# Gated linear attention into a gated SSM on one Trainium2 core: all small tiles of a turn in one cluster, TensorE's program filled to three fetch blocks a turn, loads behind the cluster

## The chip, the cores and the metric

The kernel runs on one core of one Trainium2 chip. The metric is the device time of one execution in microseconds (us); the median of three runs of the kernel before is 269.57 us (269.48 to 269.81). All views below come from one execution that the hardware profiler recorded; it took 269.61 us itself.

Engines: PE is TensorE's matmul stream (PEld its weight loads, PEq its sequencer), DVE is VectorE, ACT is ScalarE, POOL is GpSimd, SP is SyncE, which here only issues DMA.

## The reference

Two blocks follow each other, all in fp32, with B=4, H=8, S=768, D=48, 384 = H·D and 512 inner channels:

```python
# q, k, v, alpha: (B, H, S, D)
for t in range(S):
    state = alpha[:, :, t, :, None] * state + einsum('bhd,bhe->bhde', k[:, :, t], v[:, :, t])
    y[:, :, t] = einsum('bhd,bhde->bhe', q[:, :, t], state)
x = y.transpose(0, 2, 1, 3).reshape(B, S, H * D)
proj = x @ w_in                       # 384 x 1024
val, gate = proj[..., :512], proj[..., 512:]
for t in range(S):
    h = exp(A_log) * h + val[:, t, :]
    ys[:, t, :] = h
out = (gate * sigmoid(gate) * ys) @ w_out   # 512 x 384
```

## The kernel before

The 4 x 768 positions are cut into N = 12 groups of 256, three to a batch; one pass of the main loop over n is a turn. A group consists of two chunks of 128 (c) or four subchunks of 64 (u, L = 64). The recurrence of the first block is done per subchunk, in matrix form: `scan_P` forms the running product P of alpha, `scan_V` the same backwards, and with them q and k are scaled into Zq and Zk. What a turn works on is spread over three groups: turn n projects group n, finishes the attention of group m = n+1, and starts that of m+1.

TensorE's work in a turn, in the order of before:

- `project(n, cc)` for cc = 0..3 (L989): the product of x with w_in, 24 matmuls 128x128 by 128x256, each run as two passes. Each cc gives a half pv (the value) and a half pg (the gate). DVE scans pv into hh (L996), ACT makes silu of pg (sg, L1007), and POOL multiplies the two into f_last (L1009).
- `third(m)`: products of Zq with the carried state sums (`carried`, L848) and of the masked scores with v within a subchunk pair (`values(m, False)`, L835); `join` then copies y to yst and moves it by DMA into xT, the next projection's right-hand side.
- `scores(m+1)` (L799): 64 matmuls of 48x64 by 48x112 in two halves, of Zk with Zq; the result is masked by DVE (L814) into A and copied by ACT to AK, of which POOL masks a part (L819), and to K.
- `output_parts(n)` (L1072): the product of f with w_out by seven instead of eight half-products (S1 to S4, T1 to T4 are sums of quarters of f and of w_out). S3 and S1 (L1056, L1059) are made on POOL, S2 (L1060) and S4 (L1061) on DVE, behind the last f; DVE (L1100 to 1102) and POOL (L1098, L1103) combine the products. It is a generator: each `next(outs)` issues a piece.
- `second(m+1)`, issued at the head of the next turn: `values(m+1, True)` (L835) and `states` (L867), behind which ACT evicts the states and POOL adds them up (`add_up`, L885, L887).

The stages for 48x64 and 64x64 tiles are called small below; projection and outputs use full 128x128 tiles. In a turn of before there are two clusters of small work: third with scores, and, behind the outputs, values with states.

DVE's preparations for later groups come from the generator `products(l)`, of which `go(k)` issues the next k steps: transpose of alpha (al, L601), of k, `scan_P` (L636), a junk read on ACT with `scan_V` (L655), Zk (L620), transpose of q, Zq (L611). No scheduler reorders anything: instructions run on each engine in the order in which this code issues them (`manual_schedule`). Which PSUM bank a product gets is written out by hand, as a string of digits (`taken`).

The first turns (n = 0, 1) have an order of their own; the diff's main part is the branch of n >= 2.

Of the kernel before, what the change touches and what calls it, by code (L numbers as in the profile page):

```python
# [343 lines left out]
FLOOR = 1e-31  # L344


@with_exitstack
def fast(
# [128 lines left out]
    As, Ks = [A0, AK[:, :, :, D:]], [K0, AK[:, :, :, 0:L]]  # L477
# [184 lines left out]
    def products(m):  # L662
# [21 lines left out]
                 "23012301" "230132" "01230123" "012310" "23012301" "230132" "01230123" "012310"  # L684
                 "23012301" "230132" "01230123" "012310" "23012301" "230132" "01230123" "012310"
                 "23012301" "0132" "01320132" "0132")

    def bank(tag=None):
        if tag:
            return ps_at.tile([C, 512], FP32, tag=tag, name=tag)  # L690
        return ps_mm.tile([C, 512], FP32, tag=f"mm{next(taken)}", name="mm")
# [111 lines left out]
    def masks(m, cs=range(G), between=None):  # L803
        sc = [[t[:, 0:4 * (L + D)].rearrange("p (h x) -> p h x", h=4) for t in pair] for pair in scs[m]]
        mb = mask[:, None, :]
        if m < NG:
            for c in cs:
                for i in range(2):
                    nc.vector.tensor_mul(As[i][:, c], sc[c][i][:, :, D:], mb.to_broadcast([C, 4, L]))
                for i in range(2):  # L810
                    nc.scalar.activation((K0, dS[m % 2][1])[i][:, c, :, 0:D], sc[c][i][:, :, 0:D], AF.Copy)
            return
        for c in range(G):
            nc.vector.tensor_mul(A0[:, c], sc[c][0][:, :, D:], mb.to_broadcast([C, 4, L]))  # L814
            nc.scalar.activation(AK[:, c], sc[c][1], AF.Copy)  # L815
        if between:
            between()
        t = AK.rearrange("p c h x -> p (c h) x")[:, :, D:]
        nc.gpsimd.tensor_mul(t, t, mb.to_broadcast([C, G * 4, L]))  # L819
        for c in range(G):  # L820
            nc.scalar.activation(K0[:, c, :, 0:D], sc[c][0][:, :, 0:D], AF.Copy)

    def values(m, across):

        v_sb = vs[m % NV]
        if across:
            ys[m] = [t.rearrange("p (e t) -> p e t", e=2) for t in bank_pair("y")]
        for c in range(G):
            for e in range(2):
                for h in range(2):  # L830
                    i = 1 - h if across else h
                    for s in range(2):
# [3 lines left out]
                                         v_sb[rows, c, 4 * i + p, :], As[i][rows, c, p, :],  # L836
# [15 lines left out]
    def states(m):  # L852
# [7 lines left out]
        for c in range(G):  # L860
            for p in range(4):
                for h in range(2):
                    if c < n[h]:
                        rows = ds(L * h, L)
                        for i in range(2):
                            to = st[h][ds(64 * i, D), c, p, :] if m else st[h][c][ds(64 * i, D), p, :]
                            nc.tensor.matmul(to, ((K0, dS[m % 2][1]) if m < NG else Ks)[i][rows, c, p, 0:D],  # L867
# [6 lines left out]
        for h in range(2):  # L874
            nc.scalar.activation(parts[h][:, 0:n[h], :, 0:D], st[h][:, 0:n[h]], AF.Copy)  # L875
# [99 lines left out]

    def project(n, cc, late=False, between=None):
# [10 lines left out]
        def passes(part):  # L987
            for vg, kk in part:
                nc.tensor.matmul((pv, pg)[vg], w_ins[cc][:, kk, vg, :], xT[:, kk, :],  # L989
                                 start=(kk == 0), stop=(kk == NK - 1))  # L990

# [83 lines left out]
    def output_parts(n):  # L1075
# [11 lines left out]
        yield  # L1087
# [125 lines left out]
    def second(m):  # L1213
        if m < N:
            values(m, True)
            states(m)
            add_up(m, (0, 1, 2))

    def third(m):
        if m < N:  # L1220
            carried(m, (1,))
            values(m, False)
            carried(m, (0, 2, 3))
            return join(m, [nc.sync, nc.gpsimd])

    late = (1,)
    for n in range(N):
# [37 lines left out]
        elif n == 1:  # L1265
# [29 lines left out]
            f2()  # L1295
            output(0)
# [8 lines left out]
        else:  # L1305
            if n == 2:
                first(m)
            if n - 1 not in late:
                go(1)
                if n == N - 2:  # L1310
                    check_w(5)
                next(outs, None)
                second(m)
                go(1)
                if n == N - 2:
                    check_w(0)
            else:
                go(1)
            f0 = project(n, 0)
            f0()  # L1320
            if n == N - 2:
                check_w(1)
            if n == 2:
                go(1)
            load_raw("a", n + 3, nc.sync)
            load_raw("k", n + 3, nc.sync)
            if n != 2:
                go(1)
# [3 lines left out]
            if n - 1 in late:  # L1332
                second(m)
            if n == 2:
                go(1)
# [10 lines left out]
            load_raw("q", n + 3, nc.sync)  # L1346
# [3 lines left out]
            f3 = project(n, 3)  # L1350
            f3()
            if m + 1 < N:
                go(1)
# [6 lines left out]
            rest = third(m)  # L1360
            if n < N - 1:
                outs = output_parts(n)
            if n not in late and m + 1 < N:
                scores(m + 1)
                masks(m + 1, between=lambda: next(outs))
                next(outs)
                rest()
                add_up(m, (3,))
                next(outs)
                go(1)  # L1370
                if n == N - 3:
                    check_w(4)
            else:
                if m < N:
                    next(outs)
                    next(outs)
                    rest()
                    add_up(m, (3,))
                if n < N - 2:
                    go(1)  # L1380
                    for _ in outs:
                        pass
            load_v(m + 2, nc.sync)
# [4 lines left out]
        if n == N - 2:  # L1388
            for _ in outs:
                pass  # L1390
        if n > 1 and n in late:
# [54 lines left out]
```

## Time and profile before

| quantity | value |
|---|---|
| median of three runs | 269.57 us (269.48 to 269.81) |
| the profiled execution | 269.61 us |
| its span, first to last instruction | 267.9 us |
| granted TensorE clock | 1.000 |
| DMA packets, moved | 52304, 41.19 MB |

Lines of the profile name the engine, the line of the code, the operation and out<-in by the program's names. "busy" is the time in which an engine's instructions ran, and what stands in brackets behind a timeline row is the engine's idle time ahead of it and what released it. q8 is the queue that brings instructions. In the chain of waits, each row is a piece of the chain: start in us, length in us, engine, tile and line, and the number of passes.

The busy tenths of PE and POOL in 40 slices of the span show the shape of the run: a ramp, the steady turns, and an end in which POOL has less to do.

```profile
PE   7999999999999999999999999999999999999994
POOL 8221314084168997995985995996876986646010
```

### The profile page before, as it was taken

To read this page: it belongs to the slowest core of one execution; us is meant where nothing else is said; L and a number is where in the kernel's file an instruction comes from. 1 tells how busy PE (TensorE), PEld (TensorE's weight loads), DVE (VectorE), ACT (ScalarE), POOL (GpSimd) and SP (SyncE) were. 2 spreads that over 40 slices of the span, in tenths; PEclk is the share of its full clock that TensorE was granted. 3 is DMA by queue.
4 is the path that set the end of the run, shared out by engine and by line. 5 is a ranking of instruction groups with operands and counts; after the bars stand their busy time and mean duration, and the time that the engine had idled before them with its cause. 6 is when DMAs were issued, how large, how long until landed. Compare 5 with 4: busy or idle time off the path is not lost.

```text
span 267.9 us, 10005 instructions
## 1 busy us (share of the span) xinstructions
PE 262.4 (98%) x4172; PEld 230.5 (86%) x4172; DVE 236.9 (88%) x326; ACT 111.9 (42%) x272; POOL 166.0 (62%) x186
## 2 busy tenths in 40 slices
PE   7999999999999999999999999999999999999994
PEld 5998889877688988988988988988988989988984
DVE  7979998996999999999999998999999998883462
ACT  4667766372242642532533524524524515214021
POOL 8221314084168997995985995996876986646010
PEclk9999999999999999999999999999999999999999
DMA  5948984896993669559697488569598501201101
GB/s 177 307 141 262 287 187 152 227 209 149 271 219 82 133 164 223 122 146 221 132 230 165 104 218 184 125 160 216 128 209 174 144 2 29 76 2 38 68 7 60
DMA packets 52304, 41.19 MB, mean 154 GB/s; under 512 B 27392, under 2 KB 50944, under 8 KB 52256
## 3 DMA queue, kind: packets, MB, share of 16 engines
q1 hardware_dynamic: 49472, 37.53, 57.8%
q0 software_dynamic: 1536, 2.20, 3.2%
q10 hardware_dynamic: 1248, 0.79, 1.1%
q8 instruction: 34, 0.56, 0.9%
q14 instruction: 14, 0.11, 0.1%
HBM read 32.54 MB, written 4.72 MB: 139 GB/s over the span
## 4 chain that ended last, share of the span: by engine, by line
PE 91%; DVE 2%; DMA 2%; issue 1%; ACT 1%; POOL 1%; ACTq 0%; DVEq 0%; POOLq 0%
PE mm L989 47%; PE mm L1072 18%; PE y L835 4%; PE y L848 4%; PE mm L1023 4%; PE s L799 4%; PE mm L799 3%; PE s L867 3%; DMA raw_q<-in_q_dram 2%; PE mm L708 1%; PE mm L704 1%; PE mm L703 1%; DVE P L636 1%; PE mm L751 1%; POOL w_in L557 1%
## 5 line engine op out<-in xcount | busy, mean ns | idle before, releaser
L989 PE MATMUL mm<-xT,w_in 128*128 128x256 f32 x576 | 129.2, 382 | 0.1
L989 PEld LDWEIGHTS mm<-xT,w_in 128*128 128x128 f32 x576 | 108.0, 190 | 15.8 <-POOL w_in L557 0.4
L1007 ACT ACTIVATE sg<-mm 128x256 f32<-128x256 f32 x48 | 18.4, 383 | 88.8 <-PE mm L989 84.4
L1009 POOL TENSOR_TENSOR f_last<-sg,hh 128x256 f32<-128x256 f32 x36 | 28.3, 794 | 26.1 <-ACT sg L1007 22.6
L887 POOL TENSOR_TENSOR sum<-sum,dS 128x192 f32<-128x192 f32 x30 | 39.7, 1325 | 3.0 <-ACT dS L875 1.4
L636 DVE TENSOR_TENSOR_SCAN P<-al,lower 128x1028 f32<-128x1028 f32 x12 | 30.7, 2562 | 0.3
L996 DVE TENSOR_TENSOR_SCAN hh<-a_dec,hh,mm 128x256 f32<-128x256 f32 x32 | 23.3, 729 | 8.3 <-PE mm L989 7.8
L655 DVE TENSOR_TENSOR_SCAN V<-al,ends 128x1028 f32<-128x1028 f32 x12 | 28.5, 2375 | 0.4
L964 POOL DMA_DIRECT2D xT<-yst x44 | 22.5, 517 | 5.1 <-ACT yst L961 3.7
L557 POOL TENSOR_TENSOR w_in<-w_in,wr 128x768 int32<-128x768 int32 x4 | 7.3, 1823 | 25.5 <-DVE wr L552 16.1
L1072 PE MATMUL mm<-wide,wr 128*128 128x192 f32 x120 | 23.0, 327 | 0.0
L1072 PEld LDWEIGHTS mm<-wide,wr 128*128 128x128 f32 x120 | 20.0, 190 | 0.0
L601 DVE STREAM_TRANSPOSE k<-raw_k 128x1024 f32<-128x1024 f32 x9 | 18.5, 2054 | 0.0
L601 DVE STREAM_TRANSPOSE q<-raw_q 128x1024 f32<-128x1024 f32 x9 | 18.3, 2030 | 0.0
L875 ACT ACTIVATE dS<-s 128x384 f32<-128x384 f32 (+1 forms) x18 | 7.4, 461 | 24.4 <-PE s L867 24.4
L1072 PE MATMUL mm<-w_out,f_last 128*128 128x192 f32 x80 | 17.4, 340 | 0.0
L819 POOL TENSOR_TENSOR AK<-AK,mask 128x512 f32<-128x512 f32 x9 | 13.7, 1522 | 5.9 <-ACT AK L815 5.7
L601 DVE STREAM_TRANSPOSE al<-raw_a 128x1024 f32<-128x1024 f32 x8 | 16.4, 2052 | 0.0
L620 DVE TENSOR_TENSOR Zk<-k,V 128x1024 f32<-128x1024 f32 (+1 forms) x14 | 16.0, 1146 | 0.3 <-ACT k L715 0.3
L611 DVE TENSOR_TENSOR Zq<-q,P 128x1024 f32<-128x1024 f32 (+1 forms) x14 | 15.7, 1120 | 0.0
L848 PEld LDWEIGHTS y<-Zq,sum 48*64 48x64 f32 x656 | 11.6, 134 | 3.5 <-issue 3.2
L835 PE MATMUL y<-A,v 64*64 64x64 f32 x352 | 14.5, 221 | 0.0
(196 smaller groups left out, 502.5 us busy)
## 6 DMA issues: line engine op xcount, KB each, us to landing
out_dram<-o_sb SPq DMA_DIRECT2D x23, 192.0 KB, 2.3
v<-in_v_dram SPq DMA_DIRECT2D x22, 192.0 KB, 4.1
raw_k<-in_k_dram SPq DMA_DIRECT2D x18, 184.0 KB, 5.2
raw_q<-in_q_dram SPq DMA_DIRECT2D x18, 184.0 KB, 5.4
raw_k<-in_k_dram SPq DMA_DIRECT2D x18, 176.0 KB, 5.4
raw_q<-in_q_dram SPq DMA_DIRECT2D x18, 176.0 KB, 5.4
wbits<-in_moe_w_in_dram SPq DMA_DIRECT2D x8, 384.0 KB, 4.9
raw_a<-in_alpha_dram SPq DMA_DIRECT2D x16, 184.0 KB, 3.9
```

Of the source, the lines that this page charges most:

```text
L601: nc.vector.transpose(out=by_runs(to).rearrange("p h c j -> p h j c"), in_=raws[name][:, 0:4 * ROW].rearrange("p (h j d) -> p h j d", h=4, ...
L636: nc.vector.tensor_tensor_scan(out=P, data0=al[:, 0:4 * GP], data1=lower.rearrange("p h t -> p (h t)"), initial=0.0, op0=ALU.mult, op1=ALU ...
L655: nc.vector.tensor_tensor_scan(out=V[:, ::-1], data0=al[:, 1:4 * GP + 1][:, ::-1], data1=ends.rearrange("p h t -> p (h t)")[:, ::-1], init ...
L799: nc.tensor.matmul(scs[m][c][i][ds(L * h, L), ds(p * (L + D), L + D)], Zk[rows, c, p, ds(h * L, L)], Zq[rows, u, p], start=True, stop=True ...
L835: nc.tensor.matmul(ys[m][i][ds(64 * s, 64), e, ds(c * C + h * L, L)], v_sb[rows, c, 4 * i + p, :], As[i][rows, c, p, :], start=across and ...
L848: nc.tensor.matmul(ys[m][i][ds(64 * s, 64), e, ds(u * L, L)], Ss[j][rows, p, :], Zqs[m % 2][rows, u, p, D:], start=False, stop=True, skip_ ...
L887: nc.gpsimd.tensor_add(Ss[j][:, :, 0:D], Ss[j - 1][:, :, 0:D], part)
L964: engines[n % len(engines)].dma_start(out=xT[to, a], in_=st[rows, i, e])
L989: nc.tensor.matmul((pv, pg)[vg], w_ins[cc][:, kk, vg, :], xT[:, kk, :], start=(kk == 0), stop=(kk == NK - 1))
L996: nc.vector.tensor_tensor_scan(out=hh, data0=a_dec[:, cc:cc + 1].to_broadcast([C, GC]), data1=pv, initial=prev_h[cc][:, GC - 1:GC] if n % ...
L1009: f = lambda: engine.tensor_mul(fs[n][cc], sg, hh)
L1072: nc.tensor.matmul(o, a[:, k], b[k] if type(b) is list else b[:, k], start=start and k == 0, stop=k == KC - 1, skip_group_check=True)
```

## The change

The order of a turn is changed, the program of PE gets empty instructions, and the loads move.

- **Order.** Behind project cc = 3 come `scores(m+1)` with its masks, then `third(m)`, and in the same cluster `states(m+1)` and `values(m+1, True)`; then the outputs. For m = 5 and 8 (`apart`) values and states stay behind the outputs. `states` hands back its eviction, issued behind an output piece; `add_up` follows.
- **Empty instructions.** `fill` spreads `FILL[n]` NO_OPs over the 24 projection matmuls of turns 1 to 9, 989 in all.
- **Buffers.** A0 and AK alternate between two places each (the second in wobits[0]); POOL's mask is two instructions, one behind each of ACT's copies; y and mm banks are handed out from one string, with "a" and "b" for the y banks.
- **Loads.** k for a later group at the head of the turn, v behind the last piece of the outputs of the turn before, q and alpha behind the cluster.
- **DVE.** Zq is ahead of the last hh, V behind the first hh.

```diff
+FILL = {1: 78, 2: 79, 3: 128, 4: 128, 5: 96, 6: 128, 7: 128, 8: 96, 9: 128}
...
+    def A_of(m):
+        n = m % 2 if m > NG else 1
+        return A0s[n], AKs[n][:, :, :, D:]
...
         for c in range(G):
-            nc.vector.tensor_mul(A0[:, c], sc[c][0][:, :, D:], mb.to_broadcast([C, 4, L]))
-            nc.scalar.activation(AK[:, c], sc[c][1], AF.Copy)
-        if between:
-            between()
-        t = AK.rearrange("p c h x -> p (c h) x")[:, :, D:]
-        nc.gpsimd.tensor_mul(t, t, mb.to_broadcast([C, G * 4, L]))
-        for c in range(G):
+            nc.vector.tensor_mul(A0s[m % 2][:, c], sc[c][0][:, :, D:], mb.to_broadcast([C, 4, L]))
+            nc.scalar.activation(AKs[m % 2][:, c], sc[c][1], AF.Copy)
             nc.scalar.activation(K0[:, c, :, 0:D], sc[c][0][:, :, 0:D], AF.Copy)
+            t = AKs[m % 2][:, c, :, D:]
+            nc.gpsimd.tensor_mul(t, t, mb.to_broadcast([C, 4, L]))
...
-            ys[m] = [t.rearrange("p (e t) -> p e t", e=2) for t in bank_pair("y")]
+            ys[m] = [t.rearrange("p (e t) -> p e t", e=2) for t in bank_pair("y" if m <= NG else None)]
...
+    def fill(n, cc, i):
+        count = FILL.get(n, 0)
+        at = 2 * NK * cc + i
+        return count * (at + 1) // 24 - count * at // 24
...
                 nc.tensor.matmul((pv, pg)[vg], w_ins[cc][:, kk, vg, :], xT[:, kk, :],
                                  start=(kk == 0), stop=(kk == NK - 1))
+                for _ in range(fill(n, cc, NK * vg + kk)):
+                    nc.tensor.nop(hint="fill", nofuse=True)
...
-    late = (1,)
+    apart = (5, 8)
...
             if n == 2:
-                first(m)
-            if n - 1 not in late:
                 go(1)
-                if n == N - 2:
-                    check_w(5)
+            else:
+                if m + 1 < N:
+                    go(1)
+                    load_raw("k", n + 3, nc.sync)
+                go(1)
                 next(outs, None)
-                second(m)
-                go(1)
-                if n == N - 2:
-                    check_w(0)
-            else:
-                go(1)
+                load_v(m + 1, nc.sync)
+            if n == N - 2:
+                check_w(5)
             f0 = project(n, 0)
             f0()
+            go(1)
...
-            f3 = project(n, 3)
+            h3, f3 = project(n, 3, True)
+            if m + 1 < N:
+                go(1)
+            h3()
             f3()
             if m + 1 < N:
-                go(1)
+                scores(m + 1)
+                masks(m + 1)
...
-            rest = third(m)
-            if n < N - 1:
+            if m < N:
+                rest = third(m)
+                load_raw("q", n + 3, nc.sync)
+                if m + 1 < N and m not in apart:
+                    evict = states(m + 1)
+                    values(m + 1, True)
+                go(1)
+                if n + 3 < N:
+                    load_raw("a", n + 4, nc.sync)
+                rest()
                 outs = output_parts(n)
-            if n not in late and m + 1 < N:
-                scores(m + 1)
-                masks(m + 1, between=lambda: next(outs))
                 next(outs)
-                rest()
-                add_up(m, (3,))
+                if m + 1 < N and m not in apart:
+                    evict()
                 next(outs)
-                go(1)
...
+                if m in apart:
+                    values(m + 1, True)
+                    states(m + 1)()
+                if m + 1 < N:
+                    add_up(m + 1)
```

How the instructions move, first on DVE around the end of a turn, from the transpose of q on. Before (L601 is the transpose, L611 Zq, L996 hh, L1060 S2, L1061 S4, L814 the masks, L636 P):

```order
L601 STREAM_TRANSPOSE q<-raw_q 128x4x8x32
L996 SCALAR_TENSOR_TENSOR hh<-a_dec,mm 128x256
L611 TENSOR_TENSOR Zq_117<-q,P 128x4x4x64
L996 SCALAR_TENSOR_TENSOR hh<-a_dec,mm 128x256
L601 STREAM_TRANSPOSE al_130<-raw_a 128x4x8x32
L1060 TENSOR_TENSOR wr<-f_last,wr 128x256
L1061 TENSOR_TENSOR wr<-f_last,wr 128x256
L814 TENSOR_TENSOR A_114<-s_2520,mask 128x256
L814 TENSOR_TENSOR A_114<-mm,mask 128x256
L601 STREAM_TRANSPOSE k<-raw_k 128x4x8x32
```

The same place of the change (L613 the transposes, L623 Zq, L1019 hh, L831 the masks into the second A, L1083 and L1084 S2 and S4):

```order
L1019 SCALAR_TENSOR_TENSOR hh<-a_dec,mm 128x256
L613 STREAM_TRANSPOSE q<-raw_q 128x4x8x32
L623 TENSOR_TENSOR Zq_117<-q,P 128x4x4x64
L1019 SCALAR_TENSOR_TENSOR hh<-a_dec,mm 128x256
L831 TENSOR_TENSOR wobits_104<-s_3097,mask 128x256
L831 TENSOR_TENSOR wobits_104<-mm,mask 128x256
L1083 TENSOR_TENSOR wr<-f_last,wr 128x256
L1084 TENSOR_TENSOR wr<-f_last,wr 128x256
L613 STREAM_TRANSPOSE al_130<-raw_a 128x4x8x32
L613 STREAM_TRANSPOSE k<-raw_k 128x4x8x32
```

Zq stands directly behind q's transpose, and the transpose of al, S2 and S4 have moved from ahead of the masks to behind them.

Then PE at the end of the projection in the change (L1010 the projection's matmuls, L816 the scores, whose place was taken by third before):

```order
L1010 MATMUL mm<-xT,w_in_99 128x256
L1013 NO_OP x5
L1010 MATMUL mm<-xT,w_in_99 128x256
L1013 NO_OP x6
L816 MATMUL s_2322<-Zq_117,Zk 64x112
L816 MATMUL s_2323<-Zq_117,Zk 64x112
L816 MATMUL s_2322<-Zq_117,Zk 64x112
```

Behind every projection matmul stand five or six empty instructions, and the first product behind the projection reads Zq of the group two turns ahead.

More of the change, by code (lines that the diff above doesn't have):

```diff
@@ L1295, in fast @@
             f2()
+            check_w(4)
             output(0)
@@ L1387, in fast @@
             output(n)
[L1388 to L1391, printed above, removed]
             first(m + 1)
```

77 lines of the change are left out of this document (31 added, 46 removed), and 5 rows, old and new, of the table taken.

## Prediction

> **What bounds the kernel now.** I read the page first: the busy shares, the chain that ended last and the queues.
>
> ```profile
> span 267.9 us, 10005 instructions
> PE 262.4 (98%) x4172; PEld 230.5 (86%) x4172; DVE 236.9 (88%) x326; ACT 111.9 (42%) x272; POOL 166.0 (62%) x186
> PEclk9999999999999999999999999999999999999999
> q8 instruction: 34, 0.56, 0.9%
> PE 91%; DVE 2%; DMA 2%; issue 1%; ACT 1%; POOL 1%; ACTq 0%; DVEq 0%; POOLq 0%
> ```
>
> TensorE (PE) is busy for 98% and holds 91% of the chain at full clock, VectorE (DVE) is busy for 88%. An 88% over the whole span hides the ramp and the tail, so next come the busy times over seven steady turns, from the start of scores(4) to that of scores(11), and over three single turns.
>
> ```profile
> 86.58:224.28 137.70, 137.70 (x2269) 124.07 (x2264) 132.78 (x149) 54.74 (x140) 113.85 (x120) 1.00 0.69 156
> sum 58.98, PE 58.98 PEld 53.15 DVE 56.59 ACT 23.36 POOL 48.12; mean PE 19.66 PEld 17.72 DVE 18.86 ACT 7.79 POOL 16.04
> ```
>
> The columns of the first row are the window, its length and then PE, PEld, DVE, ACT, POOL. PE never stops: 137.70 of 137.70, 19.67 us a turn. But DVE works 132.78 of those 137.70, so it has only 4.92/7 = 0.70 us of slack a turn. PE is the bound with a second engine right behind it. Anything that ties the two more tightly must be held against that 0.70.
>
> What PE does in one turn is read from the chain of waits (start, length, what), and what DVE does from its timeline (start, length, line, operands).
>
> ```profile
> 107.86 4.75 PE mm L1072 x28
> 112.61 0.62 PE y L835 x32
> 113.23 0.70 PE s L867 x48
> 113.94 10.56 PE mm L989 x48
> 124.49 0.39 PE y L848 x16
> 124.89 0.47 PE y L835 x32
> 125.35 0.70 PE y L848 x48
> 126.05 0.77 PE s L799 x32
> 126.82 0.77 PE mm L799 x32
> ...
> 145.56 0.77 PE s L799 x32
> ```
> ```profile
> 127.64 0.42 DVE L814 TENSOR_TENSOR A<-mm,mask 128x256 f32<-128x256 f32 x1 [0.18 <-PE mm L799]
> 127.98 2.05 DVE L601 STREAM_TRANSPOSE k<-raw_k 128x1024 f32<-128x1024 f32 x1
> 129.87 2.69 DVE L636 TENSOR_TENSOR_SCAN P<-al,lower 128x1028 f32<-128x1028 f32 x1
> 138.70 2.02 DVE L601 STREAM_TRANSPOSE q<-raw_q 128x1024 f32<-128x1024 f32 x1
> 140.58 0.66 DVE L996 TENSOR_TENSOR_SCAN hh<-a_dec,hh,mm 128x256 f32<-128x256 f32 x1
> 141.18 1.17 DVE L611 TENSOR_TENSOR Zq<-q,P 128x1024 f32<-128x1024 f32 x1
> 142.98 0.75 DVE L996 TENSOR_TENSOR_SCAN hh<-a_dec,hh,mm 128x256 f32<-128x256 f32 x1 [0.63 <-PE mm L989]
> 143.64 2.04 DVE L601 STREAM_TRANSPOSE al<-raw_a 128x1024 f32<-128x1024 f32 x1
> 145.56 0.42 DVE L1060 TENSOR_TENSOR wr<-f_last,wr 128x256 f32<-128x256 f32 x1
> 146.02 0.84 DVE L1061 TENSOR_TENSOR wr<-f_last,wr 128x256 f32<-128x256 f32 x1
> 146.78 0.41 DVE L814 TENSOR_TENSOR A<-s,mask 128x256 f32<-128x256 f32 x1
> ```
>
> The reader is to see where the slack lies: once before the last hh (0.63, for the projection) and once before the second mask (0.18, for the scores). From the second mask at 127.64 to the end of Zq at 142.35 DVE runs 14.71 us without a gap. And Zq ends at 142.35, while the scores that read it start at 145.56, after the projection and third: this lead of 3.2 us is what the change spends.
>
> **The merged cluster.** Values and states used to be a small cluster of their own between outputs and projection. Changing tile size costs PE: values took 0.62 behind outputs and 0.47 inside a cluster, 0.15 more. For the way back, the last turn's projection, with no small tile ahead of it, gives the number:
>
> ```profile
> 242.45 0.39 PE y L848 x16
> 249.07 7.12 PE mm L989 x33
> 249.94 9.50 PE mm L989 x44
> 259.44 4.99 PE mm L1072 x28
> ```
>
> 44 passes in 9.50 are 0.216 a pass, so 48 take 10.36, and a projection behind small tiles takes 10.56: 0.20 more. A cluster less saves 0.15 + 0.20 = 0.35 us. Six turns are merged (groups 4, 5, 7, 8, 10, 11 by the change's own index, all but 6 and 9): 6 x 0.35 = **−2.1 us**, if PE stays the bound. A merged turn on PE alone would be 19.66 − 0.35 = 19.31.
>
> **The scores brought forward.** In the order of before, PE ran third (0.39 + 0.47 + 0.70 = 1.56) between the projection and the scores; now the scores are right behind the projection, and their masks come ahead of S2, S4 and the al transpose on DVE. So DVE's work that used to cover PE's third and scores now stands behind the masks, and while PE computes scores, DVE has only hh and the first mask. That closes a loop through both engines: Zq, scores, second mask, all the rest of DVE's turn, Zq again. Its length, step by step:
>
> - second mask to the end of Zq, the unbroken stretch: 14.71
> - S2 and S4, now inside it (145.56 to 146.78): 1.22
> - al's transpose, now inside it (143.64 to 145.56): 1.92
> - Zq directly behind q rather than behind an hh: q ends at 140.72 and the hh started at 140.58, so that overlap is lost: 0.14
> - both halves of scores, 0.77 + 0.77 and some 0.05 for the change of tile: 1.59
> - two handovers, Zq to PE and PE to mask (126.82 + 0.77 to 127.64 is 0.05): 0.10
>
> The sum is 19.68 us a turn, against PE's 19.31. The hh and first mask cost nothing extra: 0.66 + 0.37 lies inside the 1.69 of scores and handovers, the rest of it, 0.66, is DVE idling. The loop alone is back at the pace of before: the 0.35 saved on PE is gone. Behind the waiting scores stand, on PE, third, states, values and the outputs; all become late by the wait, and join's copies and the output evictions on ACT with them, but none of these is in the loop.
>
> **Collisions with GpSimd.** On top come DVE and POOL in each other's way. S2 and S4 are the same operation on tiles of one size; the view of their line shows minimum, median and maximum in ns:
>
> ```profile
> L1060 DVE TENSOR_TENSOR wr<-f_last,wr x9: 424/426/480, 88.0 to 243.8; 128x256 f32<-128x256 f32 x9
> L1061 DVE TENSOR_TENSOR wr<-f_last,wr x9: 424/836/840, 88.5 to 244.2; 128x256 f32<-128x256 f32 x9
> L636 DVE TENSOR_TENSOR_SCAN P<-al,lower x12: 2277/2544/3274, 6.4 to 208.4; 128x1028 f32<-128x1028 f32 x12
> 134.26 2.07 POOL L885 COPY sum<-dS 128x192 f32<-128x192 f32 x1 [0.64 <-ACT dS L875]
> ```
>
> S4 is 424 alone and 836 beside POOL's S1; P is 2277 to 3274, which I put down to POOL too; a POOL copy of 128x192 takes 2.07 while V runs. The Trainium skill, page "SBUF — State Buffer", section "SBUF: two separate sides", says that VectorE with two SBUF inputs and GpSimd hold their shared port exclusively, one waiting for the other's whole instruction; these three rows agree. In the changed order S2 and S4 meet POOL's S1 and two mask pieces, P meets wide_S and the sums. The best case, both freed, is S4 −0.42 and P 2.69 − 2.28 = −0.41: −0.8 a turn. The worst is S2 doubled too (+0.42) and P at its longest (3.27 − 2.69 = +0.58): +1.0. I take +0.4, one more doubled operation, since the splitting of POOL's mask puts one more POOL instruction next to DVE's two SBUF operations. A merged turn is then 20.1 us.
>
> **The apart turns.** Two of the seven loops hold a group that stays apart (5 and 8 as index m): PE pays the change of tile there (0.35), so the projection's first part is later, and hh of its first block, which now stands ahead of V, waits for it. I take +0.3: 20.4.
>
> **Loads, buffers, banks.** Second A and AK, the y banks' use, moved loads: no engine time is added. A load is read once in some 20 us and lands in 3.9 to 5.4 (queue rows: KB, us to landing):
>
> ```profile
> raw_q<-in_q_dram SPq DMA_DIRECT2D x18, 184.0 KB, 5.4
> raw_a<-in_alpha_dram SPq DMA_DIRECT2D x16, 184.0 KB, 3.9
> ```
>
> The k load moves to the head of the turn, v behind the outputs' last part, q behind the join's DMAs, all on SP's queue, each still well ahead of its reader in the order. I take 0; the worst, one landing time of 5.4 in one turn, would still lie within the forecast's own range. The V scan behind hh does not change the length of the loop.
>
> **The empty instructions.** 989 of them on PE's program, 5.3 for each of 24 matmuls a turn. The nearest row is PE's own semaphore instruction:
>
> ```profile
> L989 PEldq EVENT_SEMAPHORE  x37: 51/51/51, 22.0 to 248.6; - x37
> ```
>
> 5.3 x 51 = 272 ns, and a projection matmul (two passes) takes 432: hidden under the matmuls already queued; **0**. Should the sequencer not run ahead, all show: 989 x 0.051 = +50 us. I take 0, as PE's semaphores cost no gap in the row of the seven turns. What the fill is for, fetch, costs nothing before: 34 blocks, and PE 137.70 of 137.70 busy. The Trainium skill, page "Runtime: NRT & Kernel Launch", section "Instruction fetch mechanics", says the engine fetches its next block while it executes and that crossing a block is mostly hidden; by that rule fill and cluster alike are worth 0 and the sum stays as it is.
>
> **The sum.** Seven loops: 5 x 20.1 + 2 x 20.4 = 141.3, against 137.70: +3.6. The first scores wait behind Zq once, +0.1. The last merged group lies behind the last scores: −0.35. Together +3.3 on the profiled execution's span of 267.9: 271.2; with the 1.7 us outside the span (269.61 − 267.9), 272.9. The median of the runs is 0.04 below that execution. Forecast: **273.0 us**. Its own range follows from the collision bounds. At +0.0 in the five merged loops and 20.1 in the apart ones: 5 x 19.68 + 2 x 20.1 = 138.6, so +0.9 + 0.1 − 0.35, 270.3. At +1.0 everywhere: 5 x 20.68 + 2 x 20.98 = 145.4, so +7.7 − 0.25, 277.0.
>
> **The rivals.**
>
> *PE stays the bound* (the other side). If the collisions fall by 0.4 or more a turn (S4 free of S1), the loop is 19.68 − 0.4 = 19.28, under PE's 19.31; then the −2.1 stands: 267.5 (two apart turns then stay on PE too). For it: S4 collides in nearly every turn now, and 0.4 is one such collision. Against it: the POOL pieces move with S2 and S4, not away from them.
>
> *A wash.* Collisions as now and apart turns no dearer than merged ones: 7 x 19.68 = 137.8, +0.1 + 0.1 − 0.35: 269.5. For it: nothing in the loop is new work; against it: it needs two terms at zero at once.
>
> *Fetch stalls in the large cluster.* Scores, third, states and values are 480 instructions in 1.54 + 1.56 + 0.70 + 0.47 = 4.3 us: 9 ns each, where the projection needs 216 ns for two. A block of 256 goes by in 2.3 us; the q8 row gives 0.9% x 16 x 267.9 / 34 = 1.1 us of transfer for one. For it: the margin is thin, and the change shapes the program by blocks. Against it: 34 blocks and no gap. Price: one transfer's 1.1 a turn over six turns, in part under the DVE loop: some +3 on the forecast, 276.
>
> *The empty instructions are not hidden:* 269.6 + 50 = 320. Or they never reach the chip: then q8 stays at 34 packets, and nothing else moves, since they are costed at 0.
>
> **How the numbers follow.** The forecast 0.55, PE as the bound 0.22, the wash 0.10, fetch stalls 0.07, the empty instructions' price 0.06. A measurement of this kernel can tell about 0.2%, 0.5 us, from no change. Faster 0.22, same 0.10, slower 0.68. The range that should hold the time reaches down over the rival on the other side and up over the forecast's own bounds and the first fetch stalls: 267.2 to 277.0.
>
> **What would show it.** Right: PE's busy share of the steady turns falls below 100%, with PE's scores waiting for DVE's Zq, DVE idling some 0.3 to 0.7 before the masks, and the turn at 20 us; values inside the cluster at 0.47, and six projections at 10.36; q8 at 34 + 989/256, about 38 packets; the projection's passes still 0.216. Wrong: PE at 100% in the steady turns (collisions fell), gaps on PE inside the cluster with no engine as releaser (fetch), or projections longer than 10.56 (empty instructions). S4 at 424 in the changed trace would mean that the collision term has the wrong sign.

## The result and the profile after

The changed kernel takes 283.83 us (median of four runs, 283.43 to 284.6), the kernel before 269.52 us on the same chip: ratio 1.0534, interval 1.0507 to 1.0562. The forecast of slower holds, but the loss is 14.3 us where 3.4 were forecast, and the time lies outside the range. The profiled execution of the changed kernel took 284.6 us with a span of 282.9, against 267.9 before.

The page of the changed kernel: busy shares, the queue that brings instructions (packets, MB, share), and the chain.

```profile
PE 264.6 (94%) x4172; PEld 232.7 (82%) x4172; DVE 238.6 (84%) x326; ACT 112.6 (40%) x272; POOL 158.9 (56%) x195
q8 instruction: 37, 0.61, 0.9%
PE 52%; DVE 30%; issue 6%; DMA 6%; ACT 2%; SPq 1%; POOL 1%; DVEq 0%; ACTq 0%; POOLq 0%
```

PE's chain share fell from 91% to 52%, DVE's rose from 2% to 30%, and 6% is "issue": an engine that waits for nothing the profile shows. The same seven turns as in the prediction, scores(4) to scores(11) (window, length, then PE, PEld, DVE, ACT, POOL):

```profile
86.46:236.52 150.06, 138.50 (x2245) 124.94 (x2245) 133.37 (x147) 55.37 (x140) 107.41 (x126) 1.00 0.65 147
```

They take 150.06 instead of 137.70 us, 12.36 more of the span's 15.0. PE works 0.8 longer and stands still for 11.56, where it never did. PE's waits over the whole span (what waited, for what: us in total, times, longest) tell it in two parts:

```profile
PE s L816 <- DVE Zq L623: 4.4, 8, 0.8
PE mm L862 <- issue: 4.2, 4, 1.3
PE y L862 <- issue: 3.9, 4, 1.1
PE mm L1095 <- issue: 0.4, 1, 0.4
PE y L1095 <- issue: 0.4, 1, 0.4
```

The first row is the wait that the prediction forecast, eight times, 0.55 us each. The two L862 rows are a stop that it had costed at nothing: 8.1 us, eight times, in the middle of third. (The two rows of 0.4 us lie in the outputs of the two apart turns, at no block's end, and come back in many runs below; they are not counted as stops.) The chain of one merged turn shows where (start, length, what):

```profile
105.92 1.24 DVE Zq L623
107.16 0.14 issue
107.30 1.00 PE s L816 x32
108.29 0.77 PE mm L816 x32
109.06 0.23 PE mm L862 x16
109.29 0.47 PE mm L849 x32
109.76 0.23 PE mm L862 x15
109.98 1.34 issue
111.33 0.70 PE mm L862 x33
112.03 0.69 PE s L881 x46
112.71 0.52 PE y L849 x32
113.24 4.75 PE mm L1095 x28
117.98 1.24 PE mm L1010 x6
119.22 5.56 DMA raw_k<-in_k_dram
```

32 + 32 + 16 + 32 + 15 = 127 passes, then 1.34 us of nothing, inside a run of equal matmuls on the same operands. It is pass 127 in all eight turns (127 passes are 254 weight loads and matmuls). The last row names a load of k, and the page's chain has 6% of DMA for such rows, but no engine is seen waiting for it: DVE, whose timeline follows, does not idle for more than 0.04 us at a time between 119.32 and 129.37. A stop also costs more than its gap: 33 carried passes behind it show 0.70 us, as many as 48 took in one piece before, and the first half of the scores behind its wait shows 1.00 instead of 0.77. That is some 0.2 us each time.

DVE's timeline behind that stop:

```profile
117.44 0.35 DVE L1122 TENSOR_TENSOR wr<-wide,mm 128x192 f32<-128x192 f32 x1 [0.36 <-PE mm L1095]
...
119.32 0.75 DVE L1019 TENSOR_TENSOR_SCAN hh<-a_dec,hh,mm 128x256 f32<-128x256 f32 x1 [0.87 <-PE mm L1010]
119.98 0.16 DVE L665 RECIPROCAL ends<-P 128x4 f32<-128x4 f32 x1
120.17 2.30 DVE L667 TENSOR_TENSOR_SCAN V<-al,ends 128x1028 f32<-128x1028 f32 x1
...
127.49 1.23 DVE L623 TENSOR_TENSOR Zq<-q,P 128x1024 f32<-128x1024 f32 x1
128.63 0.74 DVE L1019 TENSOR_TENSOR_SCAN hh<-a_dec,hh,mm 128x256 f32<-128x256 f32 x1
129.90 0.42 DVE L831 TENSOR_TENSOR wobits<-s,mask 128x256 f32<-128x256 f32 x1 [0.53 <-PE s L816]
130.66 0.42 DVE L831 TENSOR_TENSOR wobits<-mm,mask 128x256 f32<-128x256 f32 x1 [0.34 <-PE mm L816]
```

The first hh waits for PE's projection, V stands behind it, and Zk, q and Zq behind V. So PE's stop arrives at Zq, and Zq holds the next scores: a loop through both engines, 107.30 to 128.86, 21.56 us.

### Where the blocks begin

PE's records (weight loads, matmuls, empty instructions, semaphores), counted in order of start, put the stop in all eight turns exactly 256 records behind the first record of scores, its wait for Zq; the numbers of both leave 193 when divided by 256. So a block of 256 is taken to begin at each such number. Against these blocks stand the 16 KiB packets of queue q8 (one packet a block, an estimate: before, PE has 8,452 records and q8 34 packets, 249 a packet). For three blocks of the changed kernel that begin with scores, and three of the kernel before that begin in a cluster (us):

```
kernel   block starts, lasts   packet starts, takes   next block runs
after    107.19  4.14          108.43  1.42           111.33
after    128.75  3.87          130.36  0.93           132.62
after    151.29  3.75          152.40  1.38           155.04
before   104.93  2.27          104.23  1.35           107.21
before   144.16  2.28          142.85  1.38           146.44
before   183.40  2.13          179.66  1.34           185.53
```

A block of small tiles can pass in 2.1 to 2.3 us; before, its successor's packet had been started ahead of it. In the changed kernel the packet starts 1.1 to 1.6 us into the block and PE goes on 1.3 to 1.5 us after it is over. No such block lasts less than 3.6 us.

The same count over all 20 traces, the runs below included, from 25 to 260 us, gives 620 blocks, with the packets put to the blocks in their order. None begins sooner than 1.2 us after its packet is over. PE idles at 97 of the ends for 1.2 to 1.7 us after a packet; the other idling at an end is another wait, longer after the packet. Of the 82 blocks whose last record starts less than 2.75 us after their first, as only small tiles do, 19 have the next packet started at most 0.1 us into the block, and none of them ends in a stop; the other 63, with the packet 0.2 us or more into the block, all do. Of the 484 blocks of 4 us and more, 12 end in a stop.

### The profile page after: what moved, and what is told of

Read it like the earlier page. It is cut to its first block, busy times and chain, and to the rows that moved or that the text cites. A ratio compares the mean times of both kernels' runs of the same rounds, so it can differ in the third digit from the quotient of the medians.

```text
span 282.9 us, 11027 instructions
## 1 busy us (share of the span) xinstructions
PE 264.6 (94%) x4172; PEld 232.7 (82%) x4172; DVE 238.6 (84%) x326; ACT 112.6 (40%) x272; POOL 158.9 (56%) x195
## 4 chain that ended last, share of the span: by engine, by line
PE 52%; DVE 30%; issue 6%; DMA 6%; ACT 2%; SPq 1%; POOL 1%; DVEq 0%; ACTq 0%; POOLq 0%
PE mm L1010 14%; PE mm L1095 14%; DVE q L613 6%; DVE V L667 6%; DMA raw_k<-in_k_dram 5%; DVE hh L1019 5%; DVE Zq L623 4%; PE s L816 3%; PE mm L816 3%; PE y L1095 3%; PE s L881 3%; PE y L862 2%; DVE P L648 2%; PE y L849 2%; DVE Zk L632 2%
## 5 line engine op out<-in xcount | busy, mean ns | idle before, releaser
L1010 PE MATMUL mm<-xT,w_in 128*128 128x256 f32 x456 | 103.6, 382 | 0.1
L1010 PEld LDWEIGHTS mm<-xT,w_in 128*128 128x128 f32 x456 | 85.5, 190 | 12.4 <-POOL w_in L569 0.4
L1032 POOL TENSOR_TENSOR f_last<-sg,hh 128x256 f32<-128x256 f32 x36 | 40.3, 1121 | 33.1 <-DVE hh L1019 21.9
L980 POOL DMA_DIRECT2D xT<-yst x44 | 22.5, 517 | 12.7 <-ACT yst L977 12.4
L1010 PE MATMUL y<-xT,w_in 128*128 128x256 f32 x120 | 27.5, 379 | 0.0
L1019 DVE TENSOR_TENSOR_SCAN hh<-a_dec,hh,mm 128x256 f32<-128x256 f32 x26 | 19.2, 738 | 8.1 <-PE mm L1010 8.1
L1010 PEld LDWEIGHTS y<-xT,w_in 128*128 128x128 f32 x120 | 22.8, 190 | 3.1
L903 POOL TENSOR_TENSOR sum<-sum,dS 128x192 f32<-128x192 f32 x30 | 18.6, 621 | 2.0
L613 DVE STREAM_TRANSPOSE k<-raw_k 128x1024 f32<-128x1024 f32 x9 | 18.2, 2024 | 0.0
L613 DVE STREAM_TRANSPOSE q<-raw_q 128x1024 f32<-128x1024 f32 x9 | 18.2, 2024 | 0.0
L1120 POOL TENSOR_TENSOR wide_S<-wide_S,wr 128x192 f32<-128x192 f32 x9 | 15.1, 1674 | 5.6 <-ACT wr L1103 5.5
L1095 PE MATMUL mm<-wide,wr 128*128 128x192 f32 x88 | 17.2, 327 | 0.4 <-issue 0.4
L816 PEld LDWEIGHTS s<-Zq,Zk 48*64 48x64 f32 x384 | 9.6, 133 | 8.5 <-PE y L1010 3.6
L613 DVE STREAM_TRANSPOSE al<-raw_a 128x1024 f32<-128x1024 f32 x8 | 16.4, 2050 | 0.0
L816 PE MATMUL s<-Zq,Zk 48*64 48x112 f32 x384 | 11.9, 261 | 4.4 <-DVE Zq L623 4.4
L623 DVE TENSOR_TENSOR Zq<-q,P 128x1024 f32<-128x1024 f32 (+1 forms) x14 | 15.4, 1102 | 0.3
```

The lines of the kernel that those rows point to most:

```text
L613: nc.vector.transpose(out=by_runs(to).rearrange("p h c j -> p h j c"), in_=raws[name][:, 0:4 * ROW].rearrange("p (h j d) -> p h j d", h=4, ...
L623: nc.vector.tensor_mul(Zqs[m % 2][:, ds(u0, n), :, D:].rearrange("p u h t -> p h u t"), t[:, :, at].rearrange("p h (u t) -> p h u t", t=L) ...
L816: nc.tensor.matmul(scs[m][c][i][ds(L * h, L), ds(p * (L + D), L + D)], Zk[rows, c, p, ds(h * L, L)], Zq[rows, u, p], start=True, stop=True ...
L903: nc.gpsimd.tensor_add(Ss[j][:, :, 0:D], Ss[j - 1][:, :, 0:D], part)
L980: engines[n % len(engines)].dma_start(out=xT[to, a], in_=st[rows, i, e])
L1019: nc.vector.tensor_tensor_scan(out=hh, data0=a_dec[:, cc:cc + 1].to_broadcast([C, GC]), data1=pv, initial=prev_h[cc][:, GC - 1:GC] if n % ...
```

## The experiments

The expectations call a stop a hold. Four theories were on trial. **F**: PE runs out of instructions at the end of a block of small tiles. **D**: the prediction's loop through DVE alone. **D2**: the loop through both engines, closed by V's place behind the first hh. **P**: PE waits for POOL's mask. Times are medians of two to five runs (b4 of eight); the kernel before ran beside them at 269.2 to 270.2.

### Moving the blocks in the changed kernel

```diff
-FILL = {1: 78, 2: 79, ...
+FILL = {1: 94, 2: 79, ...       # a1;  1: 206 in a2;  FILL = {} in a3
```

> The changed kernel with 16 more empty instructions in turn 1, so that every later block of 256 instructions begins 16 instructions ahead of the cluster instead of with it. Theory F (fetch: the hold of 0.8 to 1.3 us behind the 127th pass of every cluster is PE out of instructions, because its sequencer stands at the wait for Zq on the first instruction of a block and asks for the next block only then): the hold moves to about pass 119 and falls below 0.5 us each, a smaller one may appear at the start of the outputs; eight holds of 8.0 us in all become at most 4; time 277 to 281. Theory P (the hold is PE waiting for POOL's mask on AK, as the view of waits puts it): hold unchanged behind pass 127, time within 0.6 of 283.8. Theory D (the loop through DVE alone sets the turn): time within 0.6 of 283.8, wherever the hold goes.

> The changed kernel with 128 more empty instructions in turn 1, so that a block ends half a block earlier. F: no hold behind pass 127; a hold of 0.8 to 1.5 us behind pass 191 or so, where the block that lies wholly in the cluster ends; time 280 to 285. P: hold stays behind pass 127, 283.8. D: 283.8 within 0.6.

> The changed kernel without any empty instruction. F: a turn is 640 or fewer instructions, the block ends fall at other passes from turn to turn, the holds with them and of other sizes; q8 back to 33 or 34 packets; time 278 to 286. P and D: holds and time unchanged, 283.8 within 0.6. If the empty instructions cost time themselves, the projection's 10.5 us becomes shorter and the time falls by more than 3.

a1: 281.99 us (280.67 to 283.31). The stop left pass 127 in every turn: one is left at pass 119, and five stand at the start of the outputs, where the next block ends. PE's waits:

```profile
PE s L816 <- DVE Zq L623: 4.7, 8, 0.9
PE mm L1095 <- issue: 3.2, 6, 1.1
PE y L862 <- issue: 0.7, 1, 0.7
PE y L1095 <- issue: 0.4, 1, 0.4
```

Without the two rows' worth of 0.4 us that the changed kernel has too, the stops are 3.5 us instead of 8.1. a2: 286.60 us, the stops stand in states, behind pass 190 or 191 (L881, 6.7 us), as worked out from half a block. a3: 282.25 us, the stops fall at six different passes (126, 142, 173, 189, 205, 237) and three lines. In all three no waiting stage moved, only the count of instructions. The waits of PEld name POOL's mask for the same stops ("PEld mm L862 <- POOL AK L835"); that reading falls, since the masks stayed where they were. a1's time is 1 us and a2's 1.6 us above what F expected. For a2 the trace shows why: 206 empty instructions in turn 1 are too many to hide, and the steps from pass to pass in that turn's projection add up to 13.00 us instead of 9.92. And a3, without any, takes no less than a1: with 240 passes, 480 instructions, in one cluster, a block that is small tiles but for some 16 instructions lies in it wherever blocks begin. The two runs of a1 (280.67 and 283.31) and of a3 (280.59 and 283.91) spread as far as their gain on the changed kernel, so what these three runs show is the place of the stops, not a price.

### V and al

```diff
+            go(1)                 # V ahead of the first hh (b1, b2, b3)
             f0 = project(n, 0)
...
             h3, f3 = project(n, 3, True)
-            if m + 1 < N:
-                go(1)
             h3()
...
                 scores(m + 1)
+                go(1)             # al ahead of the masks (a4, b3)
                 masks(m + 1)
...
-                go(1)             # a4, b3
+                if m + 1 == N:
+                    go(1)
```

> The changed kernel with al's transpose issued between the scores and the masks again, where DVE now idles 0.9 us a turn. D: the loop shortens by up to 0.9 us in each of seven or eight turns: time 276 to 279. F: the holds stay behind pass 127 as long as scores still wait for Zq; if the wait for Zq goes, the hold goes with it and the time falls below 276. P: the masks on POOL do not move, holds unchanged.

> The changed kernel with VectorE's order inside the projection as before: V ahead of the first hh, Zk between the first two, q between the second and third, Zq behind the third. Theory D2 (the turn is a loop through both engines: scores, cluster, outputs, first projection part, first hh, V, Zk, q, Zq, scores; each hold on PE lengthens it because V stands behind an hh that waits for PE): freeing V takes PE's part out of the loop, DVE's waits for hh fall below 0.5 a turn, time 274 to 278 though the fetch holds stay. Theory D (masks, S2, S4 and al behind the scores are all of it): V's place is nothing, 283.8 within 1.5. Theory F (fetch): holds behind pass 127 remain at 0.8 to 1.3, because scores still wait for Zq on a block's first instruction.

> The same with 16 more empty instructions in turn 1. D2 with F: holds fall to 4 us in all as in the run with those 16 alone, but the loop is DVE's by now: 273 to 277, not more than 2 below the run without them. If F alone set the time: 4 or more below it.

> The same two, and al's transpose again between scores and masks. With V free, DVE's 0.9 us of idling ahead of the masks is what is left of the loop: D and D2 expect it filled, PE the bound again except for its holds of some 4 us: 268.5 to 273. F without D2: as the run before it.

a4: 285.08 us, no gain. DVE's idling ahead of the masks went to zero, as D wanted, and came back as waiting for the outputs (L1122), 11.0 us instead of 0.4; for the projection (L1019) DVE waits 9.7, as much as before the edit (8.7). D alone falls. b1: 278.53 us, 0.5 over its range but 5.3 less than the changed kernel, with DVE's order in the projection as in the kernel before. PE's waits in b1:

```profile
PE y L862 <- issue: 2.9, 3, 1.3
PE mm L862 <- issue: 2.8, 3, 1.2
PE y L1095 <- issue: 0.4, 1, 0.4
PE mm L1095 <- issue: 0.4, 1, 0.4
PE s L816 <- DVE Zq L623: 0.4, 2, 0.2
```

The wait for Zq is gone (0.4 from 4.4), so D2 holds. But 5.7 us of stops remain, up to 1.3, also in turns where Zq was ready 0.9 us ahead of the scores. So F's reason, that the sequencer asks late because it stands at the wait for Zq, is not all of it. b2: 278.11, 0.4 below b1, which is within its runs' spread (277.20 to 279.03), where F alone wanted 4. b3: 276.55 us (275.76 to 277.35), the best kernel with the merged cluster, 3.6 above what was expected: 4.1 us of stops, 3.1 of them at a block's end in the outputs, and DVE's waiting for the outputs again, 9.9 us.

### Undoing the cluster and the order

```diff
-    apart = (5, 8)
+    apart = range(3, N)                   # c1, c3, c4, d1, d2, e1, e2, f1
...
-                scores(m + 1)             # c2, c3, d1, e1, e2:
-                masks(m + 1)              # behind third
...
-"23012301" "23" "23ba" "01"               # c1, c3, c4: banks of the change's apart turns
+"23012301" "23" "0132" "ab"               # d1, d2, e1, e2, f1: those of before
```

> The changed kernel with values and states behind the outputs in every turn, as it has them in two turns. D2 (loop through both engines, V behind the first hh): values, states and the change of tile, 1.5 us, come ahead of the projection again and so into the loop; six more turns of about 22.4 instead of 21.2: 288 to 293. F (fetch): the holds behind pass 127 stay, and the cluster's second block becomes harmless; by F alone 283 to 285.

> The changed kernel with third ahead of scores again, values and states still in the cluster. F: the cluster's first instructions no longer wait for Zq, so the sequencer asks for the next block earlier: holds behind pass 127 below 0.4. New waits of PE for the masks before values, 0.5 to 1.5 us a turn, since nothing lies between scores and their readers. D2: loop as long as before, with V behind the first hh. 276 to 284.

> The changed kernel with its order undone on both engines (third, scores, outputs, values and states; al ahead of the masks, V ahead of the first hh), but with its loads, second buffers, split masks, banks and empty instructions. If the order is all of it: 269 to 271.5, no waits for Zq and no holds over 0.4. If the loads, banks or empty instructions cost something too: 273 or more.

> The best run so far (V and al as before, 16 more empty instructions) with values and states behind the outputs in every turn: scores first, but no block wholly inside a cluster. F: holds vanish, PE pays the change of tile again (0.35 a turn): 270 to 273, some 4 below the run with the merged cluster. If the merged cluster is worth its saving: 277 or more.

c1: 291.52 us, as D2 had it: with values and states ahead of the projection again, the loop is longer, 22.1 us a turn. c2: 298.52 us, far over its range. Its trace has six stretches of 3.41 us at half the granted clock (0.963 in the mean), which by themselves are up to 10.2 us (6 x 3.41 / 2, an estimate); why they came is not known. No stop is left at a block's end, as F expected. With third ahead of the scores nothing lies between scores and their readers, and PE stands for them:

```profile
PE s L881 <- ACT K L833: 6.2, 6, 1.6
PE mm L1095 <- ACT K L833: 3.1, 2, 1.7
PE mm L849 <- POOL wobits L835: 1.9, 5, 0.5
PE y L849 <- POOL AK L835: 1.9, 6, 0.5
```

So the merged cluster needs third between scores and states: the two changes of order come together. c3: 290.06 us instead of 269 to 271.5 (a second run, at a granted clock of 0.971, took 295.84), but for a reason of its own: outputs took the banks of the scores (9.0 us for ACT's K). Its clock is 0.988, with two such stretches. c4: 279.76 us instead of 270 to 273: stops of 0.5 to 0.7 at pass 120 in four turns, and 0.3 to 0.4 at the outputs in all. Both missed, and both with the banks of the change's apart turns.

> Order undone on both engines (third, scores, outputs, values and states; al ahead of the masks, V ahead of the first hh) and the banks handed out as before, so that outputs do not take the banks of the scores; loads, second buffers, split masks and empty instructions stay as in the changed kernel. If order is all of the loss: 269 to 271.5, PE with no gap over 0.4 in the steady turns. If the other parts cost something: 273 or more, with gaps on PE that name it.

> Scores ahead of third, values and states behind the outputs, V and al as before, 16 more empty instructions, banks as before. If the 0.3 to 0.7 us waits of PE in the run with the change's banks came from the banks, they go at the outputs: 276 to 278, the holds at pass 120 stay. If they came from fetch alone: 279 to 281 as there.

d1: 277.70 us (ratio 1.0294, 1.0270 to 1.0318). Not 270: with the order undone, stops of 0.3 to 0.7 are left at passes 125 to 128 in five of eight turns, 2.9 us, again at the end of a block that begins with the cluster, or up to five records ahead of it, though third at its head waits for nothing. d2: 278.57 us, 0.6 over its range; the waits at the outputs went, so those were the banks, and 1.9 us of stops are left in the steady turns.

### Position alone

```diff
-FILL = {1: 78, ...
+FILL = {}                                  # e1 and f1;  1: 174 in e2
...
+FILL = {n: 128 for n in range(3, 10)}      # b4: added to the kernel before
+FILL = {2: 132, 3: 128, 4: 128, 5: 96, 6: 128, 7: 128, 8: 96, 9: 128}   # e3
```

> The kernel before with 128 empty instructions a turn in turns 3 to 9, so that its clusters start near a block's first instruction in each turn. If empty instructions and block position cost something by themselves: 273 or more. If the hold needs a wait at the block's first instruction, as F says, nothing here waits there: no hold over 0.3, 269.6 within 0.8, q8 at 37 packets.

> Order undone and banks as before, without empty instructions. If the position of the blocks makes the holds (F): block starts fall at other places from turn to turn, holds in fewer turns, 272 to 276. If it does not: holds at pass 125 to 128 stay and 277.7 within 0.6.

> Order undone and banks as before, 96 more empty instructions in turn 1, so that every block that holds a cluster's start begins 96 instructions ahead of it and no block is made of small tiles alone. F: no holds over 0.3, 272 to 275, 3 to 5 below the run without these 96. Otherwise 277.7 within 0.6.

> The kernel before with empty instructions counted so that a block begins with the first instruction of third in turns 3 to 9, nothing else changed. F: a hold of 0.4 to 1.0 behind about pass 127 of the cluster, that is, inside scores, in most of these turns, which the run with 128 a turn did not have: 273 to 277. If position alone is nothing: 269.6 to 272.

b4: 271.80 us, ratio 1.0064 (1.0029 to 1.0100), one stop of 0.6. F had wanted 269.6 within 0.8 and none over 0.3. Still, 896 empty instructions cost 0.6% where no block is made of small tiles alone (the shortest lasts 4.3 us). e3 has 964 of them, as dense, and the order of before, but a block begins 26 to 28 records into third: 282.58 us, ratio 1.0513 (1.0445 to 1.0581), nearly as much as the whole change and 5.6 over its expectation. Its chain, one turn:

```profile
107.42 0.77 PE s L800 x32
108.19 0.37 PE mm L800 x13
108.56 2.23 issue
110.79 0.79 PE mm L800 x19
```

Six such stops, all behind pass 140 or 141, make 7.9 us of the span's 12.2. A stretch of 3.41 us at half the granted clock (0.994 in the mean) is up to 1.7 of the rest (an estimate, half of it). e1, the order undone without empty instructions: 273.80 us (ratio 1.0148, 1.0129 to 1.0166), 3.9 less than d1, and no stop that the blocks make. Its waits:

```profile
PE mm L1095 <- ACT wobits L832: 0.8, 1, 0.8
PE mm L1095 <- ACT wide L1103: 0.2, 1, 0.2
PE mm L1010 <- DVE hh L1019: 0.2, 1, 0.2
```

e2, with 96 more: 276.42 us, no stop in the clusters, one of 0.6 in a projection, and turns as in e1 (19.7 to 20.1); its steady turns bear F out. Its total lies 1.4 over the expectation, in the turns ahead of them: with 174 empty instructions in turn 1 the steps of that projection add up to 11.25 us instead of 9.92, and the stop of 0.6 stands there too.

### The scores' place by itself

> Scores ahead of third, values and states behind the outputs, V and al as before, banks as before, no empty instructions. If fetch holds and V's place were the loss, the scores' place adds little to the run that differs only in it (273.8): 273 to 275.5, waits for Zq below 0.3 a turn. If DVE's loop of the prediction (0.4 a turn over before) is real by itself: 276 or more, with waits for Zq in most turns.

f1: 274.75 us (ratio 1.0171, 1.0148 to 1.0194), 1.0 over e1, with one stop of 0.9 and no wait for Zq. Scores ahead of third cost little as long as V and al stand as before.

## Why the prediction failed, point by point

- **The wait for Zq** was right in place, and near in size: forecast DVE idling 0.3 to 0.7 ahead of the masks, measured 0.53 to 0.59 and 0.34 ahead of the two masks; PE's waits for Zq 0.3 to 0.8. The loop can be redone on the turn shown. From the second mask (109.10) to the end of Zq (128.72) are 19.62 us, of which DVE idles 0.36 and 0.87; 18.39 are its own work, and the prediction's terms give 14.71 + 1.22 + 1.92 + 0.14 = 17.99, with its 0.4 for collisions 18.39. So DVE's part had the right length, to the hundredth by luck (see the collisions). What failed is that the stretch is not unbroken: 1.23 us of waiting for PE lie in it, and from Zq's end to the second mask it is 1.94 instead of 1.69.
- **"Fetch costs nothing".** This step failed first. The part on the empty instructions set fetch at 0, because no stop is seen before and by the rule that it cites. The prediction had worked out that a block of the cluster passes in 2.3 us against 1.1 us of transfer and called the margin thin. The transfer is not all that counts: the packet starts 1.1 to 1.6 us into the block, and PE goes on only 1.3 to 1.5 us after its end. From the block's start to the next block's first instruction it is 3.6 to 4.1 us. The stops are 8.1 us of PE's standing still and some 0.2 each for the restart, and in e3, where only empty instructions were added, the kernel before becomes 12.7 us slower, 7.9 of them stops. As a rival it had 0.07 and +3 us, and its sign, gaps on PE inside the cluster with no engine as releaser, is what came. The Trainium skill, page "Runtime: NRT & Kernel Launch", section "Instruction fetch mechanics", says that crossing a block is mostly hidden. The traces agree for long blocks, where 12 of 484 end in a stop, and not for blocks of small tiles, where 63 of 82 do.
- **"The V scan behind hh does not change the length of the loop."** This failed as well. It is the link through which PE's cluster, its stops, the outputs and the first projection part enter DVE's loop. Undone alone (b1) it gives 5.3 us back, and the wait for Zq goes. That the loop through DVE would hold a turn at 20.1 us with V ahead is not shown: b1's turns are 20.69 in the mean, longer than that.
- **Collisions.** Forecast +0.4 a turn. Measured medians on the changed kernel, ns:

```profile
L1083 DVE TENSOR_TENSOR wr<-f_last,wr x9: 416/571/589, 88.6 to 258.6; 128x256 f32<-128x256 f32 x9
```
```profile
L1084 DVE TENSOR_TENSOR wr<-f_last,wr x9: 425/829/834, 89.2 to 259.1; 128x256 f32<-128x256 f32 x9
```
```profile
L648 DVE TENSOR_TENSOR_SCAN P<-al,lower x12: 2223/2280/2599, 7.1 to 223.0; 128x1028 f32<-128x1028 f32 x12
```

  S2 426 to 571, S4 836 to 829, P 2544 to 2280: together −0.1. For these three the sign was wrong. DVE's whole stretch came out 0.40 longer all the same, by small differences elsewhere; that the turn is 21.56 instead of 20.1 is due to the two steps above.
- **The merged cluster** on PE was right: the projection behind it takes 10.36 (117.98 to 128.34, where the last pass ends 0.52 before 128.86), values 0.52 against 0.62. Less the 0.22 and 0.23 of restarts, and the 1.34 and 0.52 of waiting, the turn's 21.56 is 19.25 of PE, forecast 19.31. Nothing of it reaches the end, since PE is not the bound.
- **The apart turns** were forecast 0.3 over the merged; the two are 22.54 and 22.28 against 20.8 to 21.6. The first hh waits 2.36 there.
- **Empty instructions** are hidden, and cheaper than their nearest row: 13 ns each, not 51. That holds at the 5.3 a matmul of this kernel; 7.3 (e2) and 8.6 (a2) in turn 1 add 1.3 and 3.1 us to its projection. q8 has 37 packets, 38 were forecast.

```profile
L1013 PEldq NOP  x989: 13/13/13, 49.0 to 234.8; - x198
```

Stepwise, each a run (differences under 1 us are within the runs' spread): changed kernel 283.8; V back 278.5; 16 more empty instructions 278.1; al back 276.6; cluster split, banks of before, 278.6; no empty instructions 274.8; scores behind third 273.8; the kernel before, 269.5 to 269.9.

**What stays open.** The last 3.9 us: e1 loses about 1.6 in its first such turn (21.32 us against 19.74, where the outputs wait for ACT) and 0.1 to 0.35 in others, with ACT copying both K ahead of the outputs; that this order on ACT, the split masks or the moved loads is the cause was not tried. What makes the sequencer ask for a block early (before) or late (changed) is not settled either: the wait for Zq at a block's first instruction goes with the late ones, but b1, d1 and e3 have stops without it. What is shown is only that a block of small tiles ends in a stop when the next packet starts after the block does. No kernel tried is faster than the one before.

## What to carry to other kernels

Count instructions, not only time: a stretch of small tiles that runs 256 instructions in less than about 4 us can stop TensorE at the end of its block (in these traces each block under 2.75 us did whose next packet started 0.2 us or more into it, and late packets stopped blocks of up to 6.8 us too), and joining two such stretches, to save 0.35 us of changing tiles, made a whole block of them. Before an operation is moved behind one that waits for another engine, follow what stands behind it round to that engine. And an "issue" gap inside a run of equal matmuls, at the same pass in every turn, is a count; move it with empty instructions before believing the releaser that the view of waits names.

## What was not expected of the hardware

Empty instructions that cost 13 ns each and 1.6 us in b4 came with 12.7 us in e3, most of it by where they put the blocks' ends. The stops at a block's end were 0.2 to 2.6 us long. And packets of 0.9 to 1.4 us were over 1.3 to 1.5 us before PE went on.
